# A fused attention kernel planned once and traced twice, with named buffers, planned tail jobs and sums spread by transposes

## The chip, the core and the metric

The kernel runs as one program on one core of a Trainium2 chip. The metric is device time in microseconds, lower is better. The core's engines run side by side, each through its own queue in order: TensorE (PE; its weight loads, PEld, have rows of their own), VectorE (DVE), ScalarE (ACT), GpSimd (POOL), and SyncE (SP), which here only issues DMAs.

## What is computed

Three layers follow each other: attention in which a query sees only the keys of its hash bucket, a causal attention with four experts of which two count per token, and a token mixer with a sine and a cosine. Everything is float32; the kernel splits each operand of a matmul into a high and a low part and multiplies high by high, high by low and low by high.

```python
def _attn_ref(q, k, v, proj):                      # 2 x 8 heads, 768 tokens, 64 wide
    ...                                            # 6 sign bits of q @ proj and k @ proj give buckets
    mask = q_bucket[:, :, :, None] == k_bucket[:, :, None, :]
    scores = scale * np.matmul(q, k.transpose(0, 1, 3, 2))
    scores = np.where(mask, scores, -1000000000.0)
    ...                                            # exp(scores - max)
    attn = attn / (np.sum(attn, axis=-1, keepdims=True) + 1e-09)
    return np.matmul(attn, v)

def _moe_ref(x, w_gate, wq, wk, wv, wo):           # x: (2, 768, 512), 4 experts, 2 of them per token
    ...
    for e in range(E):                             # q, k, v = x @ wq[e], x @ wk[e], x @ wv[e]
        ...                                        # causal softmax a, with the same division by its sums
        ye = a @ v @ wo[e]
        ...                                        # out += gate weight * ye

def _moe2_ref(x, w_theta, w_tok_r, w_tok_i, w_ch):
    theta = x @ w_theta
    zr, zi = x * np.cos(theta), x * np.sin(theta)
    u = x + np.einsum('ts,bsd->btd', w_tok_r, zr) + np.einsum('ts,bsd->btd', w_tok_i, zi)
    return u + np.maximum(u @ w_ch, 0.0)
```

## The kernel before

**Stages.** `attn_units` makes 12 units for each of 4 head pairs and each of 2 batches: a unit is 128 rows of scores of one head (`scores`, L861), their minimum and scaling on DVE (`low`, L870), the exponential on ACT (`exp`, L879), six to eight transposes on PE (`flip`, L887), the high part on ACT (`split_hi`, L898), the low part on DVE (`split_lo`, L901), and for two units together the product with V (`mix`, L917). `moe_units` makes 24 like them, causal and in four groups, with the projections of the experts between (`heads_a`, L1205; `value_rows`, L1140). A "group" is a head pair or an expert pair; there are 12.

**The spread of the sums.** When a group's exponentials are done, `scale` takes the reciprocals r (128 x 12) of the row sums, and POOL splits them into three bf16 parts (rs, L653 and L803, four instructions). `spread` transposes rs on PE (L816, bf16), ACT copies the 36 x 128 result (L818), and six bf16 matmuls with a constant of ones (`pick`, L820) lay the reciprocals out as 128 x 768 in PSUM. `finish` multiplies (L828).

**The tail.** From the end of the last group's units on, each of 12 token tiles (b, i) goes through `theta` and `out_proj` (L1389, six matmuls of 512 columns each), the range reduction (ACT L1421 and L1422, DVE L1423 to L1425; L1423 is the first and last reader on DVE that frees theta's PSUM tile), `trig`, `split_z` (zh, zl), and `mix` (L1493). `slab` brings weights for the mixer, with a decoding of 64-bit words on DVE (L674 to L676) for some. theta's and out_proj's PSUM tiles are called wk from (0, 2) on and have two buffers; ACT L1396 (`out_proj`'s copy x) frees the other one. `flip_u` and `channels` (L1401, L1413) end the program. POOL makes low parts (L701), the products with sine and cosine (L1433, L1434) and the sums of two halves (L811).

**What sets the order.** The code is a list of jobs. `Plan` reads the traced program, gives each instruction a price (`price`) and lists the instructions of each engine in an order by modelled times (`arrange`, shaken by the seeds of NUDGES). It is used twice: the first trace is planned with the order of the PSUM tiles ps left free; `sequence` turns it into an order of jobs up to the tail; the program is traced again in that order, planned again with all buffers going round in the order of the trace, and `fix` nails that second plan's order to each engine. The tail's jobs are traced in the order in which they are written. `busy` puts 38 filler matmuls (L765) into gaps of the first 20 us.

## Time and profile before

| | us |
|---|---|
| median of 3 timed runs (lowest to highest) | 558.03 (557.77 to 560.16) |
| the profiled execution | 552.84 |
| its span, first to last instruction | 551.0 |
| PE busy in it | 535.4 (3413 matmuls) |
| DVE, ACT, POOL busy in it | 438.8, 375.0, 291.7 |

The profiled execution is 5.2 us below the median. Matmuls are pipelined: a row's duration is that of one instruction from start to end, while what PE needs for it is the step to the next row's start. So the step is read from start times, and "busy" is a union of overlapping durations.

### The profile page before, as it was taken

To read this page: it belongs to the slowest core of one execution; us is meant where nothing else is said; L and a number is where in the kernel's file an instruction comes from. 1 tells how busy PE (TensorE), PEld (TensorE's weight loads), DVE (VectorE), ACT (ScalarE), POOL (GpSimd) and SP (SyncE) were. 2 spreads that over 40 slices of the span, in tenths; PEclk is the share of its full clock that TensorE was granted. 3 is DMA by queue.
4 is the path that set the end of the run, shared out by engine and by line. 5 is a ranking of instruction groups with operands and counts; after the bars stand their busy time and mean duration, and the time that the engine had idled before them with its cause. 6 is when DMAs were issued, how large, how long until landed. Compare 5 with 4: busy or idle time off the path is not lost.

```text
span 551.0 us, 9682 instructions
## 1 busy us (share of the span) xinstructions
PE 535.4 (97%) x3413; PEld 464.4 (84%) x3413; DVE 438.8 (80%) x723; ACT 375.0 (68%) x693; POOL 291.7 (53%) x286
## 2 busy tenths in 40 slices
PE   7999999999999999999999999979799999999997
PEld 4989998899889889899998988967588878788886
DVE  5888888898987898788895988889939799763343
ACT  6788887888764787678985757989356476563010
POOL 7957588648604758913121303846646576965000
PEclk9999999999999999999999999999899999999999
DMA  6744355426575766357561614533335442241012
GB/s 192 186 86 134 88 158 152 135 60 183 144 247 160 246 165 184 86 143 190 138 203 40 205 61 110 158 113 106 102 103 156 135 135 96 94 113 43 20 59 94
DMA packets 30367, 71.95 MB, mean 131 GB/s; under 512 B 4360, under 2 KB 6024, under 8 KB 30320
## 3 DMA queue, kind: packets, MB, share of 16 engines
q1 hardware_dynamic: 28160, 67.85, 43.5%
q10 hardware_dynamic: 2160, 3.50, 1.7%
q8 instruction: 27, 0.44, 0.3%
q14 instruction: 20, 0.16, 0.1%
HBM read 40.73 MB, written 14.16 MB: 100 GB/s over the span
## 4 chain that ended last, share of the span: by engine, by line
PE 78%; DVE 15%; ACT 3%; DMA 2%; issue 2%; ACTq 0%; SPq 0%; DVEq 0%
PE ps L861 16%; PE O L917 15%; PE ps L887 13%; PE ps L1493 12%; PE ps L1205 4%; PE wk L1413 3%; PE wk L1389 3%; PE ps L1413 3%; PE ps L1140 2%; PE ps L1068 2%; DVE g L676 2%; DVE ss L870 2%; DVE PTl L901 2%; DVE rr L1424 1%; DVE g L675 1%
## 5 line engine op out<-in xcount | busy, mean ns | idle before, releaser
L879 ACT ACTIVATE ss<-ss,m 128x768 f32<-128x768 f32 (+3 forms) x144 | 122.0, 848 | 22.6 <-DVE ss L870 21.8
L870 DVE TENSOR_SCALAR_CACHE_REDUCE ss<-ps 128x768 f32<-128x768 f32 (+3 forms) x144 | 119.2, 841 | 22.1 <-PE ps L861 14.6
L901 DVE TENSOR_TENSOR PTl<-ps,PTh 128x768 fp32r<-128x768 f32 x120 | 116.5, 980 | 15.1 <-ACT PTh L898 14.1
L898 ACT CAST PTh<-ps 128x768 fp32r<-128x768 f32 x120 | 98.1, 819 | 38.4 <-PE ps L887 35.8
L887 PE MATMUL ps<-ident,ss 128*128 128x128 f32 x744 | 111.0, 274 | 2.1 <-DVE PTl L901 2.0
L917 PE MATMUL O<-PTl,V 128*128 128x256 f32 (+1 forms) x384 | 104.5, 296 | 0.0
L917 PE MATMUL O<-PTh,V 128*128 128x256 f32 (+1 forms) x384 | 103.6, 293 | 0.8 <-ACT PTh L898 0.8
L887 PEld LDWEIGHTS ps<-ident,ss 128*128 128x128 f32 x744 | 85.0, 140 | 6.8 <-issue 2.6
L1493 PE MATMUL ps<-zh,tok 128*128 128x512 f32 x240 | 77.8, 395 | 0.2 <-ACT tok L698 0.2
L811 POOL TENSOR_TENSOR bt<-bt,ob 64x768 f32<-64x768 f32 x23 | 43.1, 1873 | 63.5 <-DMA bt<-ob 55.3
L917 PEld LDWEIGHTS O<-PTh,V 128*128 128x128 f32 x384 | 72.5, 189 | 3.9 <-ACT PTh L898 1.0
L917 PEld LDWEIGHTS O<-PTl,V 128*128 128x128 f32 x384 | 72.6, 190 | 2.5
L861 PE MATMUL ps<-op 76*128 76x256 f32 (+5 forms) x256 | 63.9, 342 | 1.8 <-ACT op L1006 1.6
L1493 PEld LDWEIGHTS ps<-zh,tok 128*128 128x128 f32 x240 | 44.8, 188 | 10.0 <-ACT tok L698 0.7
L1493 PE MATMUL ps<-zl,tok 128*128 128x512 f32 x120 | 45.9, 394 | 0.3 <-DVE zl L1445 0.3
L861 PEld LDWEIGHTS ps<-op 128*128 128x128 f32 (+1 forms) x256 | 40.0, 191 | 5.7 <-ACT op L1006 2.0
L701 POOL TENSOR_TENSOR tok<-raw,tok 128x512 fp32r<-128x512 f32 x27 | 40.3, 1497 | 6.1 <-ACT tok L698 5.7
L879 ACT ACTIVATION_READ_ACCUMULATOR ss<-ss,m 128x1 f32 x144 | 27.4, 190 | 0.0
L1493 PEld LDWEIGHTS ps<-zl,tok 128*128 128x128 f32 x120 | 22.5, 188 | 5.5 <-DVE zl L1445 0.7
L1433 POOL TENSOR_TENSOR kk<-kk,x 128x512 f32<-128x512 f32 x12 | 18.4, 1530 | 15.9 <-ACT kk L1432 8.4
L653 POOL TENSOR_SCALAR rs<-r 128x12 bf16<-128x12 f32 x24 | 5.4, 225 | 38.7 <-DVE r L947 21.6
L861 PE MATMUL ps<-skh,op 128*128 128x512 f32 x84 | 24.4, 358 | 0.7 <-issue 0.3
(241 smaller groups left out, 1150.0 us busy)
## 6 DMA issues: line engine op xcount, KB each, us to landing
raw<-in_wtok_dram SPq DMA_DIRECT2D x18, 512.0 KB
raw<-tok_d SPq DMA_DIRECT2D x27, 256.0 KB
bt<-ob SPq DMA_DIRECT2D x24, 192.0 KB
tok_d<-g SPq DMA_DIRECT2D x18, 256.0 KB
raw<-in_vP_dram SPq DMA_DIRECT2D x8, 384.0 KB
op<-qk_d SPq DMA_DIRECT2D x16, 192.0 KB
out_dram<-o ACTq DMA_DIRECT2D x11, 256.0 KB
raw<-in_qT_dram SPq DMA_DIRECT2D x7, 384.0 KB
```

Source lines behind the costliest of these rows:

```text
L701: nc.gpsimd.tensor_sub(l, raw, f(h))
L811: engine.tensor_add(self.bt[keep], self.bt[keep], self.ob[keep, side])
L861: nc.tensor.matmul(self.sp[:, c0:c1], lhs, rhs[:, c0 - off:c1 - off], start=a == 0, stop=last)
L870: i = nc.vector.tensor_scalar(self.ss[:, off:off + w], self.sp[:, off:off + w], -0.125, NEG, op0=OP.mult, op1=OP.min, accum_out=m)
L879: e = nc.scalar.activation(self.P[:, off:off + w], self.ss[:, off:off + w], AF.Exp, bias=m, scale=-1.0, accum_out=self.grp.den[:, side, i: ...
L887: nc.tensor.transpose(self.pt[:, j * 128:(j + 1) * 128], self.P[:, j * 128:(j + 1) * 128], ident)
L898: nc.scalar.copy(self.d[0], self.v)
L901: nc.vector.tensor_sub(self.d[1], self.v, f(self.d[0]))
L917: nc.tensor.matmul(o, g.V[:, j, side, :], rhs, start=j == 0 and a == 0, stop=j == w // 128 - 1 and a == 1)
L1205: nc.tensor.matmul(pp[:, c0:c1], lhs[:, kd, e, :], rhs[kd][:, c0:c1], start=n == 0, stop=n == 3 * NK - 1)
L1413: nc.tensor.matmul(o, lhs[:, sl], rhs[:, kd, cols], start=n == 0, stop=n == 3 * NK - 1)
L1493: nc.tensor.matmul(yp[t], lhs[:, a, t, :], rhs[:, a], start=i == 0 and a == 0 and n == 0, stop=i == NT - 1 and a == 1 and n == 2)
```

## The change

The program is planned once. A `Desk` counts the tiles that each job allocates; after the plan, `homes` gives each tile of a tag with more tiles than buffers the number of the buffer that the plan chose for it, and the second trace allocates it under a tag of its own with that number (`Pool.tile`). `fix` puts the first plan's order onto the second trace's instructions. The tail (`theta`, `out_proj`, `trig`, `split_z`, `slab`, `mix`, `flip_u`, `channels`, the opening of its pool) becomes jobs that `sequence` may move. Some prices and all NUDGES are new. `load_values` is a job of its own. The spread widens r on POOL into rb (128 x 768, float32) and transposes it with six float32 transposes; the transpose, the ACT copy, the POOL splits, `count` and `pick` are gone.

```diff
 NUDGES = [
-    (4000007, 402.2, 442.2, 300), (4000009, 440.6, 450.6, 1000), (4000016, 207.4, 247.4, 300),
...
-], [
-    (12000023, 40.3, 80.3, 300), (12000029, 0, 600, 100), (12000042, 117.9, 137.9, 100),
...
+    (1000006, 101.0, 181.0, 300), (1000018, 228.8, 308.8, 300), (1000108, 411.7, 421.7, 1000),
...
+class Desk:
+    def __init__(self, homes=None):
+        self.homes = homes or {}
+        self.job, self.count, self.made, self.starts = -1, 0, {}, {}
+    def begin(self, job, at):
+        self.job, self.count = job, 0
+        self.starts[job] = at
+class Pool:
...
+    def tile(self, shape, dtype, name, tag=None, bufs=1):
+        desk = self.desk
+        desk.count += 1
+        key = desk.job, desk.count
+        if key in desk.homes:
+            t = self.pool.tile(shape, dtype, name=name, tag=f"{tag}.{desk.homes[key]}", bufs=1)
...
         if n < 30:
-            s = 170 if o.kind != "InstReciprocal" else 240
+            s = 240 if o.kind == "InstReciprocal" else 450 if o.tiles[-1].startswith("den") else 170
...
         if len(o.w) > 1:
-            s = 82 + n * 1.045
+            return 82 + n * 1.045, 202 + n * 1.045
...
     s = 45 + n * 2.3 if o.kind == "InstTensorTensor" else 165 + n * 0.82
+    s += 150 if n < 30 else 0
...
+    def homes(self, t, made, reuse):
+        slot, used = {}, {}
+        def fresh(name):
+            if name not in slot:
+                slot[name] = used.setdefault(self.tag[name], 0)
+                used[self.tag[name]] += 1
+            return slot[name]
+        for old, new in reuse:
+            slot[new] = fresh(old)
...
-    def fix(self, tc, order):
+    def fix(self, nc, tc, order, waits, before, now):
...
+        def same(n):
+            k = bisect.bisect_right(starts, n) - 1
+            i = ins[n if k < 0 else n - starts[k] + now.starts[jobs[k]]]
...
         for line in order.values():
+            line = [same(n) for n in line]
             for a, b in zip(line, line[1:]):
-                tc.add_manual_dep(self.ops[b].ins, self.ops[a].ins.name, why, reason="order")
+                tc.add_manual_dep(b, a.name, why, reason="order")
...
-    count = const.tile([36, 2, NT], F32, name="count")
...
-    pick = const.tile([36, NT, 128], BF, name="pick")
...
-            r = r.rearrange("p h i -> p (h i)")
-            self.rs = pool.tile([128, 3, 2 * NT], BF, name="rs", tag="rs", bufs=2)
-            for n in range(2):
-                hi_pool(self.rs[:, n], r)
-                nc.gpsimd.tensor_sub(r if n == 0 else self.rs[:, 2], r, self.rs[:, n])
+            self.rb = pool.tile([128, NT, 2, D], F32, name="rb", tag="rb", bufs=1)
+            nc.gpsimd.tensor_scalar(self.rb,
+                                    r.rearrange("p h i -> p i h")[:, :, :, None].to_broadcast([128, NT, 2, D]),
+                                    1.0, 0.0, op0=OP.mult, op1=OP.add)
...
             self.rp = rp = ps_tile()
-            flat = rp.bitcast(BF)[0:36, 1792:1920]
-            nc.tensor.transpose(flat, self.rs.rearrange("p a c -> p (a c)"), identb)
-            rT = pool.tile([36, 128], BF, name="rs_T", tag="rs_T", bufs=2)
-            nc.scalar.copy(rT, flat)
             for i in range(NT):
-                nc.tensor.matmul(rp[:, i * 128:(i + 1) * 128], pick[:, i], rT, start=True, stop=True)
+                nc.tensor.transpose(rp[:, i * 128:(i + 1) * 128], self.rb[:, i].rearrange("p h d -> p (h d)"), ident)
...
-            if not first:
-                self.load_values()
...
+        at(s0 - (VAL0 if first else 16), pr.load_values)
...
+    def open_left():
+        s1.close()
+        late["pool"] = opened(ctx, name="p3", side="left")
+        late["wc"] = [late["pool"].tile([128, NK, DM], F32R, name="wc" + n) for n in "hl"]
...
-                    theta(*ahead)
+                    do(theta, *ahead)
                 if what == "o" and ahead:
-                    out_proj(*ahead)
+                    do(out_proj, *ahead)
...
+    for k in sequence or range(len(jobs)):
+        fn, args = jobs[k]
+        desk.begin(k, len(nc.cur_bb.bb.instructions))
+        families[k] = family(fn, args)
+        fn(*args)
...
-    line = None
-    for last in (False, True):
+    plan = line = None
+    desk = Desk()
+    while True:
...
-                waits, turns, stages = [], [], []
-                fused(tc, *args, waits, turns, stages, line)
-                plan = Plan(nc, tc, waits, turns, () if last else FREE)
-                t, order, _ = plan.arrange(SLACK, 6, NUDGES[last])
-                if not last:
-                    line = plan.sequence(t, stages)
-                    raise Draft
-                plan.fix(tc, plan.busy(t, order, 20e3))
+                waits, turns, families = [], [], {}
+                fused(tc, *args, waits, turns, desk, families, line)
+                if plan:
+                    plan.fix(nc, tc, order, waits, before, desk)
+                    break
+                plan = Plan(nc, tc, waits, turns, FREE)
+                t, order, reuse = plan.arrange(SLACK, 6, NUDGES)
+                homes = plan.homes(t, desk.made, reuse)
+                order = plan.busy(t, order, 20e3)
+                line = plan.sequence(t, reuse, desk, families)
+                before, desk = desk, Desk(homes)
+                raise Draft
```

The planner moves instructions; three places show how. In the lists of the kernel after, lines are its own: L846 is the new transpose, L943 is L917 of before, L887 is L861 of before, L1422 is L1389, L1447 to L1449 are L1423 to L1425, L705 to L707 are L674 to L676, L1469 is L1445, L841 is L811, L854 is L828.

PE, the end of the spread of the second group (batch 0, head pair 1), before (the bf16 transpose L816 stands 19 rows ahead, and four of the six L820 directly ahead):

```order
L887 MATMUL ps<-ident,ss 128x128 x3
L820 LDWEIGHTS pick
L820 MATMUL ps<-rs_T,pick 128x128
L887 MATMUL ps<-ident,ss 128x128 x2
L917 MATMUL O<-PTl,V 128x256
L917 MATMUL O<-PTh,V 128x256
L887 MATMUL ps<-ident,ss 128x128
L917 MATMUL O<-PTl,V 128x256
L820 LDWEIGHTS pick
L820 MATMUL ps<-rs_T,pick 128x128
L861 MATMUL ps<-op,sql 128x512
```

PE, the same spread after, whole:

```order
L943 MATMUL O<-PTl,V 128x256
L846 MATMUL ps<-ident,rb 128x128 x6
L943 MATMUL O<-PTh,V 128x256
L943 MATMUL O<-PTl,V 128x256
L887 MATMUL ps<-op,sql 128x512
```

What stood in two parts, of which the second was in three runs, stands in one run; over the program the 72 L820 stand in 21 runs, beside 12 single L816, and the 72 L846 in 19.

DVE, from the range reduction of theta (0, 2) to the read that frees theta (0, 3)'s PSUM tile, before (L1423 of (0, 2) stands directly ahead; the last row is that of (0, 3)):

```order
L1424 SCALAR_TENSOR_TENSOR rr<-kk,rr 128x512
L1425 TENSOR_SCALAR rr<-rr 128x512
L674 TENSOR_SCALAR g<-g 128x512
L675 SCALAR_TENSOR_TENSOR g<-raw,g 128x512
L676 SCALAR_TENSOR_TENSOR g<-raw,g 128x512
L811 TENSOR_TENSOR bt<-bt,ob 64x768
L1445 TENSOR_TENSOR z1l<-kk,z1h 128x512
L828 TENSOR_TENSOR y<-rT,bt 128x768
L1445 TENSOR_TENSOR z1l<-rr,z1h 128x512
L674 TENSOR_SCALAR g<-g 128x512
L675 SCALAR_TENSOR_TENSOR g<-raw,g 128x512
L1423 SCALAR_TENSOR_TENSOR rr<-kk,wk 128x512
```

DVE, the same after; ahead of these rows stand L1447 of (0, 2) and then L707, L1448, L705 and L1469:

```order
L706 SCALAR_TENSOR_TENSOR g<-raw,g 128x512
L1469 TENSOR_TENSOR z1l<-rr,z1h 128x512
L707 SCALAR_TENSOR_TENSOR g<-raw,g 128x512
L1449 TENSOR_SCALAR rr<-rr 128x512
L841 TENSOR_TENSOR bt<-bt,ob 64x768
L854 TENSOR_TENSOR y<-rT,bt 128x768
L705 TENSOR_SCALAR g<-g 128x512
L706 SCALAR_TENSOR_TENSOR g<-raw,g 128x512
L707 SCALAR_TENSOR_TENSOR g<-raw,g 128x512
L1469 TENSOR_TENSOR zl<-kk,zh 128x512
L1469 TENSOR_TENSOR zl<-rr,zh 128x512
L1447 SCALAR_TENSOR_TENSOR rr<-kk,wk 128x512
```

From one such read to the next there are 12 instructions before and 16 after; from (0, 3)'s to (0, 4)'s there are 9 before and 6 after.

PE, the first use of the wk buffer that DVE frees after theta (0, 3), with the semaphores that an instruction waits for, before (wk_5283 is theta (0, 4), in the bank that theta (0, 3) had):

```order
L1493 MATMUL ps_5162<-z1l_5147,tok_5109 128x512
L1493 MATMUL ps_5162<-z1h_5146,tok_5110 128x512
L1493 MATMUL ps_5175<-z1h_5146,tok_5109 128x512 [waits Activation_49]
L1493 MATMUL ps_5162<-z1h_5146,tok_5109 128x512
L1389 MATMUL wk_5283<-wth_4586,yh_4660 128x512 [waits DVE_49]
L1389 MATMUL wk_5283<-wtl_4587,yh_4660 128x512
```

After (wk_5254 is out_proj (0, 4), in the bank that theta (0, 3) had; theta (0, 4), wk_5220, has the bank that out_proj (0, 3) had, which ACT frees):

```order
L1422 MATMUL wk_5220<-wth_4527,yl_4625 128x512
L1508 MATMUL ps_5070<-zl_5191,tok_5103 128x512 [waits DVE_49]
L1508 MATMUL ps_5083<-zh_5190,tok_5103 128x512 [waits Activation_49]
L1508 MATMUL ps_5039<-zl_5191,tok_5103 128x512
L1508 MATMUL ps_5039<-zh_5190,tok_5104 128x512
L1508 MATMUL ps_5039<-zh_5190,tok_5103 128x512
L1508 MATMUL ps_5039<-zl_5191,tok_5103 128x512 [waits DVE_49]
L1422 MATMUL wk_5254<-woh_4525,yh_4624 128x512 [waits DVE_49]
```

From theta (0, 2)'s last matmul up to the one that waits for that bank, PE has 87 matmuls before and 118 after.

## Rows read from the trace of the kernel before

**Rows 1.** The page: PE's busy time, and the chain that ended last by engine.

```profile
PE 535.4 (97%) x3413; PEld 464.4 (84%) x3413; DVE 438.8 (80%) x723; ACT 375.0 (68%) x693; POOL 291.7 (53%) x286
...
PE 78%; DVE 15%; ACT 3%; DMA 2%; issue 2%; ACTq 0%; SPq 0%; DVEq 0%
```

**Rows 2.** Busy time by stretch; columns in the first line.

```profile
core 0: us, PE busy (x) PEld busy (x) DVE busy (x) ACT busy (x) POOL busy (x), PEclk, DMA share, GB/s
0.00:10.00 10.00, 7.20 (x29) 3.42 (x30) 5.16 (x20) 5.54 (x10) 6.22 (x14) 1.00 0.61 216
...
360.00:380.00 20.00, 16.92 (x104) 13.43 (x103) 17.17 (x27) 17.75 (x33) 7.86 (x9) 1.00 0.32 108
380.00:400.00 20.00, 16.15 (x64) 12.68 (x63) 19.84 (x18) 10.19 (x19) 14.71 (x9) 0.91 0.31 88
...
440.00:460.00 20.00, 19.73 (x86) 15.85 (x85) 18.49 (x22) 14.08 (x25) 14.07 (x10) 1.00 0.30 93
```

**Rows 3.** PE's waits: who, for whom, us in total, times, longest.

```profile
PE wk L1389 <- DVE rr L1423: 3.8, 1, 3.8
PE ps L887 <- DVE PTl L901: 2.0, 1, 2.0
```

**Rows 4.** Timeline of PE around one spread: start us, duration us, instruction, count.

```profile
194.11 0.28 PE L917 MATMUL O<-PTh,V 128*128 128x256 f32 x1
194.32 0.23 PE L816 MATMUL ps<-identb,rs 128*36 128x128 bf16 x1
194.48 0.38 PE L917 MATMUL O<-PTl,V 128*128 128x256 f32 x1
194.70 0.28 PE L917 MATMUL O<-PTh,V 128*128 128x256 f32 x1
...
195.06 0.38 PE L887 MATMUL ps<-ident,ss 128*128 128x128 f32 x2
195.37 0.51 PE L820 MATMUL ps<-rs_T,pick 36*128 36x128 bf16 x6
195.81 0.66 PE L887 MATMUL ps<-ident,ss 128*128 128x128 f32 x4
```

**Rows 5.** Timeline of PE: a single L820 between transposes, and a run of six.

```profile
84.24 0.55 PE L887 MATMUL ps<-ident,ss 128*128 128x128 f32 x3
84.72 0.23 PE L820 MATMUL ps<-rs_T,pick 36*128 36x128 bf16 x1
84.88 0.44 PE L887 MATMUL ps<-ident,ss 128*128 128x128 f32 x2
...
201.90 0.82 PE L887 MATMUL ps<-ident,ss 128*128 128x128 f32 x6
```

**Rows 6.** POOL's and ACT's part of a spread, a 128 x 768 POOL copy, from groups and timelines.

```profile
L653 POOL TENSOR_SCALAR rs<-r 128x12 bf16<-128x12 f32 x24 | 5.4, 225 | 38.7 <-DVE r L947 21.6
...
364.53 0.26 ACT L818 COPY rs_T<-ps 36x128 bf16<-36x128 bf16 x1
...
13.70 0.83 POOL L653 TENSOR_SCALAR sqh<-raw 128x768 fp32r<-128x768 f32 x1
```

**Rows 7.** Timelines of PE and DVE, 359 to 396 us.

```profile
374.79 0.40 PE L1389 MATMUL wk<-wth,yl 128*128 128x512 f32 x1
...
359.88 1.94 DVE L1425 TENSOR_SCALAR rr<-rr 128x512 f32<-128x512 f32 x1
...
377.07 0.43 DVE L1425 TENSOR_SCALAR rr<-rr 128x512 f32<-128x512 f32 x1
377.42 0.68 DVE L1423 SCALAR_TENSOR_TENSOR rr<-kk,wk 128x512 f32<-128x512 f32 x1
...
395.95 0.68 DVE L1423 SCALAR_TENSOR_TENSOR rr<-kk,wk 128x512 f32<-128x512 f32 x1
```

**Rows 8.** Timeline of SP near the start: DMA issues.

```profile
2.12 0.43 SPq L969 DMA_DIRECT2D raw<-in_qT_dram  x1
...
10.63 0.46 SPq L1091 DMA_DIRECT2D skh<-skh  x1
```

More of the change, by code (lines that the diff above doesn't have):

```diff
@@ L540, in arrange, with sequence @@
         return self.forward(rank.tolist(), slack, hold=HOLD)
-    def sequence(self, t, stages):
-        starts = [s[0] for s in stages]
-        count = len(stages) - 1
-        of = [0] * len(self.ops)
-        for o in self.ops:
-            k = bisect.bisect_right(starts, o.n) - 1
-            of[o.n] = k if 0 <= k < count else None
-        pre = [set() for _ in range(count)]
+    def homes(self, t, made, reuse):
[7 more added lines that the diff above has]
+            slot[new] = fresh(old)
+        many = [key for key, (bufs, names) in self.tags.items() if len(names) > bufs]
+        homes = {made[name]: fresh(name) for key in many for name in self.tags[key][1]}
+        taken = {new for _, new in reuse}
+        self.last = max((n for key in many if key.startswith("O_") for n in self.tags[key][1] if n not in taken),
+                        key=lambda n: min(t[k] for k in self.enter[n]))
+        homes.update((made[name], slot[self.last]) for name in made if name.startswith("spare"))
+        return homes
+    def sequence(self, t, reuse, desk, families):
+        jobs = sorted(desk.starts)[:-1]
+        starts = [desk.starts[k] for k in jobs]
+        ends = starts[1:] + [desk.starts[len(jobs)]]
+        of = [bisect.bisect_right(starts, o.n) - 1 for o in self.ops]
+        pre = [set() for _ in jobs]
         def edge(a, b):
-            if a is not None and b is not None and a < b:
+            if a >= 0 and b >= 0 and a != b:
                 pre[b].add(a)
@@ L592, in sequence @@
                     heapq.heappush(heap, (when[j], j))
-        assert len(line) == count
+        assert len(line) == len(jobs), "the jobs wait for one another"
         return line
@@ L598, in busy @@
         line, ops = order["PE"], self.ops
-        waits = [[t[b] - t[a] - ops[a].step, b, 0] for a, b in zip(line, line[1:]) if t[b] < until]
+        until = min(until, min(t[n] for n in self.enter[self.last]))
+        waits = [[t[b] - t[a] - ops[a].step, b, 0] for a, b in zip(line, line[1:]) if t[b] <= until]
         step = ops[self.spare[0]].step
@@ L1416, in theta @@
     def theta(b, i):
-        th = late["work"]()
+        th = work((b, i) < (0, 2))
         project(th, b, i, "wt")
@@ L1552, in fused @@
                     if c > 1:
-                        channels(b, c - 2)
-                    flip_u(b, c)
-    late["work"] = lambda: ps_tile()[:, :DM]
+                        do(channels, b, c - 2, False)
+                    do(flip_u, b, c, False)
     b = B - 1
```

159 lines of the change are left out of this document (85 added, 74 removed), and 67 rows, old and new, of the table NUDGES.

## The prediction, made before the kernel after was run

> **What bounds the kernel now.** The page first: PE is busy for 535.4 of 551.0 us and holds 78% of the chain that ended last, with DVE next at 15% [rows 1]. So time comes off in two ways only: PE gets less to do, or PE waits less. The busy share cannot tell these apart, since overlapping durations hide small gaps; so I read steps from start to start in the timeline, and the stretches for the waits. The stretches show 3.1 us of PE idle in 360 to 380 and 3.9 in 380 to 400, where the granted clock also fell to 0.91, while DVE was busy for 19.84 of 20 us; in 440 to 460 PE takes 86 matmuls, nearly all of 512 columns, in 19.73 us, 0.23 each [rows 2]. The list of PE's waits names the two large ones: 3.8 us for DVE L1423, 2.0 us for DVE L901 [rows 3]. Before 360 us the waits that show are at the start, where PE is busy for 7.20 of the first 10 us [rows 2].
>
> **The spread, on PE.** Before, from row to row: the matmul ahead of L816 takes 0.21 in place of 0.12 (half the 0.23 of 512 columns), L816 itself 0.16, the one after it 0.22 in place of 0.12: 0.35 together. The six L820: the two transposes ahead take 0.31 in place of 0.22, the run 0.44, and the block behind it loses about 0.06 [rows 4]; 0.59 together, so 0.94 for a spread in one run, 11.3 for twelve. But the 72 L820 stand in 21 runs, nine more than needed. A single one costs 0.48 - 0.33 for three delayed transposes plus 0.16 for itself, 0.31 [rows 5], of which 0.06 is already counted: nine times 0.25 is 2.3. Sum before 13.6 us, all on PE, which sets the end. After: 72 transposes of 128 x 128 float32. A run of two lasts 0.38 [rows 4], one of six 0.82 [rows 5]: four steps more, 0.11 each; 72 x 0.11 = 7.9, and a run's ends cost nearly nothing, because the step behind the last transpose is short and the next one long by as much. Gain 13.6 - 7.9 = 5.7. Bounds: 3.4 if the nine extra runs cost nothing (11.3 - 7.9), 6.2 if each costs its whole 0.31. I take 5.7, nearest to the rows that show both forms.
>
> Here a rule of the Trainium skill speaks against the change. Runs of float32 transposes go at 0.11 a step in the rows [rows 4, 5], and 360 to 380 us, which holds one of eight, has a granted clock of 1.00 [rows 2]. The Trainium skill, page "TensorE: Matmul & The Clock Gate", section "Part 4: PE-mode transpose", says that a transpose took about 275 ns in a kernel and does not count as busy work for the clock. By its figure the 72 would be an estimated 19.8 us and the spread a loss of 6.2. The trace disagrees for the step, and shows no fall of the clock by such a run.
>
> **The spread, elsewhere.** POOL had four instructions of about 0.22 each; it gets one of 0.83, the price of a 128 x 768 copy [rows 6]: even, 0.9 against 0.8. ACT loses 12 x 0.26 [rows 6]. The chain from r to the spread loses the trip PE, ACT, PE; it was hidden behind other matmuls, so nothing but slack. Where POOL runs, DVE instructions whose operands all lie in SBUF stretch: L1425 took 0.43 at 377 us and 1.94 at 360 us [rows 7]. One rb of 0.83 can hold a DVE instruction longer than one of 0.22 did, at worst 12 x 0.6 = 7 us on DVE; DVE has slack outside 340 to 400, where two rb stand, so 0 to 1.2 on the path, and I take 0. `count` and `pick` go from the start: nothing, PE waits there for data.
>
> **Where the tail begins.** Before, theta (0, 4) took the bank of theta (0, 3) and waited for DVE L1423. PE reached it 21.9 us after theta (0, 2)'s last matmul, 3.8 of it waiting; DVE needed 18.5 us for the 12 instructions from one L1423 to the next, 1.54 each, against 0.68 for that instruction alone [rows 3, 7]. The clock then lost up to 9% of 20 us, 1.8 [rows 2]; say 5.3 in all. After, theta (0, 4) takes the bank that ACT frees, and the first to wait for that read is out_proj (0, 4), 118 matmuls on instead of 87: 104 x 0.23 + 14 x 0.12 = 25.6 us. But DVE now has 16 instructions in the place of 12: at 1.54 each 24.6, after the 2.6 from PE's last matmul to the first L1423, and 0.7 for the last [rows 7]: 27.9, so 2.3 late; at 0.68 each, not late at all. The next one is closer: theta (0, 5) needs the read of theta (0, 4), six DVE instructions later (4.1 to 9.2 us), and has 15 matmuls, 3.5 us, between: late by 0.6 to 5.7. DVE is not stretched all the way, as POOL runs dry; I take 1.5 and 0.8, no fall of the clock (the 2.0 us wait at 360 left it at 1.00 [rows 2, 3]). Gain 5.3 - 2.3 = 3.0, bounds -2.7 and 5.3.
>
> At 360 us PE waited 2.0 for an L901 that stood behind a stretched L1425 [rows 3, 7]. The plan after puts that L1425 behind two reads of scores and one L901 more. That leaves one stretched L1424 in the chain instead of two: gain 1.0, bounds 0 and 2.0.
>
> **The start.** The second head pair's q and k were issued at 2.12 us; now they stand on SP behind three moves, the last of which went out at 10.63 [rows 8]. First use was at 13.70 on POOL [rows 6]. At the 216 GB/s of the first 10 us [rows 2] 0.8 MB takes 3.6 us, so k lands near 15 and PE's hash of that pair may wait a little: loss 0.5, bounds 0 and 3. `load_values` as a job of its own moves the V loads; they land far ahead of their use: 0.
>
> **The rest of the order.** Named buffers add no instruction. Everything else is a new order of the same work; the trace shows no large wait in 20 to 340 or after 400 us to win, and a new order may bring some: 0, bounds -2 and +4.
>
> **How the numbers follow.** 5.7 + 3.0 + 1.0 - 0.5 = 9.2 off. On the profiled execution, 551.0 of span and 1.8 around it, that is 552.84 - 9.2 = 543.6. The median of the timed runs is 5.2 higher, at 558.03; the same difference gives **548.8**. A measurement tells 0.5%, 2.8 us, from no change.
>
> Case 1, the sum within about 4 us: 545 to 553, chance 0.56.
>
> Case 2, the tail's start loses all its waits (3.1 + 3.9 us and the clock's 1.5) and the spread gives its 6.2: 13 to 15 off, 542 to 545, chance 0.12. For: PE needs only DVE to keep 1.1 us per instruction there. Against: the read after next has 3.5 us of cover.
>
> Case 3, PE's gain is waited away: PE arrives sooner, but DVE and POOL do as much as before, and between 360 and 400 they set the time, not PE. Then the spreads of the last two groups give nothing and the waits for L1423 come back at their bound, 5.7 + 2.3, with the clock's 1.5 again: 5.7 + 1.0 - 0.5 - 1.0 - 9.5 + 5.3 = about 1 off, 554 to 559, chance 0.17. DVE at 19.84 of 20 us speaks for it [rows 2].
>
> Case 4, slower: the b = 0 tiles stay bound by DVE and POOL to 460 us. DVE does 22 instructions in 18.49 us in 440 to 460, 0.84 each [rows 2]; up to 0.91 each PE would not see it; at 1.2 each 22 take 26.4, 6.4 more than the stretch, and two such stretches cost 13, 4 more than all gains: from 561, and up to 570, chance 0.09. It decides if POOL runs without a pause there; before, its busy time was 14.07 of 20.
>
> Case 5, the transposes of the spread pull the clock down to its lower level, 1.2 GHz: 0.22 a step, 72 x 0.22 = 15.8 against 13.6, so 2 lost instead of 5.7 won: 556 to 557, chance 0.02. The page named above would have it so.
>
> Case 6, the change doesn't do what it says: the second trace's named buffers make waits that the plan did not know, and the order is kept by PE at the price of those; 1 to 3 us back of case 1, 551 to 555, chance 0.04.
>
> Faster by over 0.5% (below 555.2): 0.56 + 0.12 + 0.04 and a third of case 3, **0.77**. Within: the rest of case 3 and case 5, **0.14**. Slower: **0.09**. The range **542 to 557** leaves out half of case 3, case 4 and the far sides of the others.
>
> **What would show it.** The timeline of a spread: runs of L846 at 0.11, no pause ahead of them; PE's summed steps down by 5 to 6 us in 0 to 350. Waits of PE: theta (0, 4) none, out_proj (0, 4) and theta (0, 5) some 2 us for DVE, clock 1.00 in that stretch. Near 21 us a short wait for POOL. The prediction is wrong if a wait of over 3 us stands where none was, or if the spread's transposes wait for rb.

## The result

The changed kernel took 540.41 us (median of 4 runs, 539.64 to 541.77), the kernel before 558.45 beside it (557.77 to 560.16): ratio 0.9675, 95% interval 0.9644 to 0.9707. That is 18.0 us off, where 9.2 were forecast and 542 was the range's lower end. Its profiled execution took 540.96 us (span 539.2) and stands among its timed runs. Before, the profiled execution stood 5.2 us below the median. Between the two profiled executions the gain is 11.9 us, so 6 of the 18 us are in neither profile.

The page of the changed kernel, busy time (engine, us, share of the span, instructions) and the chain that ended last, as in [rows 1]:

```profile
PE 528.5 (98%) x3401; PEld 467.7 (87%) x3401; DVE 441.5 (82%) x722; ACT 371.6 (69%) x681; POOL 290.6 (54%) x249
...
PE 82%; DVE 11%; DMA 3%; issue 2%; ACT 1%; SPq 0%; ACTq 0%; DVEq 0%
```

Some of its stretches, as in [rows 2] (us; busy time and instructions of PE, PEld, DVE, ACT, POOL; granted clock, DMA share, GB/s):

```profile
0.00:10.00 10.00, 8.37 (x31) 4.30 (x32) 6.36 (x19) 5.72 (x10) 4.87 (x12) 1.00 0.44 141
...
260.00:280.00 20.00, 18.34 (x136) 16.79 (x135) 17.72 (x40) 14.76 (x34) 3.65 (x2) 0.91 0.50 145
...
360.00:380.00 20.00, 19.87 (x109) 16.74 (x108) 16.85 (x24) 15.93 (x28) 10.88 (x9) 1.00 0.33 86
380.00:400.00 20.00, 20.00 (x88) 16.16 (x87) 19.59 (x20) 13.81 (x25) 14.77 (x10) 1.00 0.40 118
...
440.00:460.00 20.00, 19.76 (x89) 16.05 (x88) 19.50 (x22) 13.71 (x25) 16.29 (x11) 1.00 0.45 136
```

What PE waited for, as in [rows 3] (total us, times, longest):

```profile
PE ps L887 <- DVE PTl L927: 2.0, 2, 1.7
PE ps L887 <- DVE ss L896: 1.2, 1, 1.2
PE ps L788 <- DVE warm L792: 1.2, 1, 1.2
PE wk L1422 <- DVE rr L1447: 0.7, 1, 0.7
PE ps L1229 <- DVE x L854: 0.6, 1, 0.6
PE ps L887 <- DVE r L973: 0.5, 1, 0.5
```

Where the tail begins PE hardly waits: 19.87 and 20.00 us busy in place of 16.92 and 16.15, the clock at 1.00 in both stretches, though DVE is about as full as before (19.59 of 20). The wait of 3.8 us for L1423 is gone; the line that answers to it, L1447, has 0.7. New are 1.7 us for an L927 at 266 us and 1.2 for an L896 at 343 us. Behind the one at 266 the granted clock fell here too: it is 0.91 in 260 to 280, which is up to 1.8 us.

To set work against waits I took PE's steps from start to start. The work in a step is the median, in the trace of before, of the steps between the same kinds of instruction; what a step takes beyond that is wait, and a lower clock counts as wait too. In us, with the waits split at the last product with V, where the tail is left alone:

| profiled execution | work | waits up to there | waits behind |
|---|---|---|---|
| before | 524.9 | 14.5 | 7.2 |
| after | 517.8 | 14.6 | 2.3 |

So the two profiles show 7.1 us less work and 4.9 less waiting in the tail. Each holds one stretch of 20 us at a clock of 0.91, up to 1.8 us that counts as wait: before in the tail (380 to 400), after ahead of the split (260 to 280). Without these the tail's waits fell by 3.1 and those ahead of it by 1.7. How finely the kinds are told apart moves work against wait: with kinds by shape and type, taken two in a row, the gain in work is 5.3 us, taken three in a row 7.5; the sums and the waits behind hardly move (7.7 and 2.9 in place of 7.2 and 2.3). So a difference of work is known to some 2 us. This table is continued below.

### The profile page after: what moved, and what is told of

The parts are those of the page before. It is cut to its first block, busy times and chain, and to the rows that moved or that the text cites. A ratio compares the mean times of both kernels' runs of the same rounds, so it can differ in the third digit from the quotient of the medians.

```text
span 539.2 us, 9655 instructions
## 1 busy us (share of the span) xinstructions
PE 528.5 (98%) x3401; PEld 467.7 (87%) x3401; DVE 441.5 (82%) x722; ACT 371.6 (69%) x681; POOL 290.6 (54%) x249
## 4 chain that ended last, share of the span: by engine, by line
PE 82%; DVE 11%; DMA 3%; issue 2%; ACT 1%; SPq 0%; ACTq 0%; DVEq 0%
PE ps L1508 15%; PE ps L887 15%; PE O L943 15%; PE ps L913 13%; PE ps L1229 4%; PE wk L1422 4%; PE wk L1437 4%; PE ps L1437 3%; PE ps L1164 3%; PE ps L1092 2%; DVE ss L896 2%; DVE g L706 2%; DVE g L705 1%; PE ps L846 1%; DVE PTl L927 1%
## 5 line engine op out<-in xcount | busy, mean ns | idle before, releaser
L896 DVE TENSOR_SCALAR_CACHE_REDUCE ss<-ps 128x768 f32<-128x768 f32 (+3 forms) x144 | 119.0, 840 | 19.1 <-PE ps L887 14.6
L927 DVE TENSOR_TENSOR PTl<-ps,PTh 128x768 fp32r<-128x768 f32 x120 | 116.2, 979 | 10.6 <-ACT PTh L924 9.9
L913 PE MATMUL ps<-ident,ss 128*128 128x128 f32 x744 | 109.8, 274 | 0.6 <-DVE ss L896 0.3
L943 PE MATMUL O<-PTh,V 128*128 128x256 f32 (+1 forms) x384 | 103.5, 293 | 0.0
L943 PE MATMUL O<-PTl,V 128*128 128x256 f32 (+1 forms) x384 | 103.5, 295 | 0.0
L1508 PE MATMUL ps<-zh,tok 128*128 128x512 f32 x240 | 78.9, 394 | 0.0
L841 POOL TENSOR_TENSOR bt<-bt,ob 64x768 f32<-64x768 f32 x23 | 43.2, 1878 | 60.6 <-DMA bt<-ob 29.7
L943 PEld LDWEIGHTS O<-PTh,V 128*128 128x128 f32 x384 | 72.8, 190 | 1.9 <-ACT PTh L924 0.3
L943 PEld LDWEIGHTS O<-PTl,V 128*128 128x128 f32 x384 | 72.8, 190 | 1.7
L887 PE MATMUL ps<-op 76*128 76x256 f32 (+5 forms) x256 | 63.5, 345 | 4.1 <-DVE PTl L927 2.0
L887 PEld LDWEIGHTS ps<-op 128*128 128x128 f32 (+1 forms) x256 | 41.0, 194 | 8.2 <-DVE PTl L927 2.4
L831 POOL TENSOR_SCALAR rb<-r 128x768 f32<-128x768 f32 x12 | 10.0, 834 | 59.0 <-DVE r L973 31.8
L706 DVE SCALAR_TENSOR_TENSOR g<-raw,g 128x512 uint32<-128x512 uint32 x26 | 25.6, 986 | 0.5
L707 DVE SCALAR_TENSOR_TENSOR g<-raw,g 128x512 uint32<-128x512 uint32 x26 | 25.5, 979 | 0.5
```

Source lines behind the costliest of these rows:

```text
L706: nc.vector.scalar_tensor_tensor(gu, words[:, :, 0], 29, gu, op0=OP.logical_shift_right, op1=OP.bitwise_or)
L841: engine.tensor_add(self.bt[keep], self.bt[keep], self.ob[keep, side])
L887: nc.tensor.matmul(self.sp[:, c0:c1], lhs, rhs[:, c0 - off:c1 - off], start=a == 0, stop=last)
L896: i = nc.vector.tensor_scalar(self.ss[:, off:off + w], self.sp[:, off:off + w], -0.125, NEG, op0=OP.mult, op1=OP.min, accum_out=m)
L913: nc.tensor.transpose(self.pt[:, j * 128:(j + 1) * 128], self.P[:, j * 128:(j + 1) * 128], ident)
L927: nc.vector.tensor_sub(self.d[1], self.v, f(self.d[0]))
```

## Experiments

### The missing 6 us: the kernel before once more

**The kernel before, unchanged.**

> The kernel before, unchanged, timed and profiled once more. In the first measurement its profiled execution took 552.84 us and its timed ones 557.77 to 560.16. Theory A (the profiled execution was a lucky one; something in before varies or waits by about 5.5 us in most executions): timed runs near 558 again, and a profiled execution near 558 too, which then shows one wait or one stretch at a lower granted clock of about 5 us that the first profile lacks. Theory B (being profiled shortens this kernel, by whatever): timed near 558, profiled near 553 again, spans of the timed runs 5 us above the profiled one's. If timed runs come to 553 here, the difference was the chip's and the ratio of the two kernels is nearer 0.977 than 0.9675.

Measured: 555.76 us (10 runs, 554.60 to 558.14) and 556.06 for 18 more runs beside it, 552.03 to 559.71. The mean granted clock of PE goes with the time: the quickest run of the 18 (552.03) had 0.997, those near 555 had 0.987 to 0.991, and 559.58 and 559.23 had 0.981; 0.016 of clock goes with 7.6 us. It isn't the whole of the scatter, for 0.984 stands beside 557.07 and beside 559.71. The first profiled execution, at 0.996, was one of the quickest that this kernel has. The first four timed runs, 558.45, lay high themselves: in this and the later groups of runs before took 555.8 to 557.1, so some 2 of the 18 us are the draw. The clock of those four runs is not on record; in the groups where it is, all but one of the runs over 557.7 had 0.981 to 0.988. The profile of this run has the same two waits, 2.0 and 3.8 us, and a lower clock behind both:

```profile
360.00:380.00 20.00, 17.45 (x89) 13.57 (x90) 14.30 (x26) 14.90 (x29) 4.43 (x8) 0.83 0.18 60
380.00:400.00 20.00, 16.16 (x66) 12.78 (x66) 19.80 (x16) 11.37 (x20) 16.24 (x10) 0.96 0.32 102
400.00:420.00 20.00, 20.00 (x85) 16.22 (x85) 10.10 (x13) 11.44 (x21) 11.73 (x9) 0.96 0.33 106
```

In the timeline of PE (start us, us, instruction, idle before it) the step of a product of 512 columns is 0.23 ahead of the wait and 0.43 for some 3 us behind it, the lower of the clock's two levels (1.2 GHz), then 0.23 again:

```profile
393.29 0.40 PE L1493 MATMUL ps<-z1l,tok 128*128 128x512 f32 x1
393.52 0.86 PE L1493 MATMUL ps<-z1h,tok 128*128 128x512 f32 x3
398.23 0.80 PE L1389 MATMUL wk<-wth,yh 128*128 128x512 f32 x1 [3.84 <-DVE rr L1423]
398.82 0.63 PE L1389 MATMUL wk<-wtl,yh 128*128 128x512 f32 x1
399.24 0.63 PE L1389 MATMUL wk<-wth,yl 128*128 128x512 f32 x1
...
402.68 0.39 PE L1493 MATMUL ps<-z1l,tok 128*128 128x512 f32 x1
402.91 0.39 PE L1493 MATMUL ps<-z1h,tok 128*128 128x512 f32 x1
```

So Theory A holds as to the scatter, though its 558 did not come, neither timed nor profiled (554.60), and the forecast's step "the same difference" is an error. By the granted clock this profile loses 0.17, 0.04 and 0.04 of 20 us, 5.0; the first lost 1.8.

**The waits filled, order kept.** The program is traced a third time, and the order of the second plan is put onto it with these extra products:

```diff
+        self.fill = {3817: 17, 4099: 16}   # instruction's number in the program: repeats ahead of it
```

> The kernel before with its order kept on every engine, and its two large waits of PE filled: 17 repeats of a V product (128 x 256) ahead of the wait at 360 us and 16 repeats of a token product (128 x 512) ahead of theta (0, 4), so PE is busy where it waited, and nothing becomes earlier. The repeats are added into the sums, so those sums hold one product 17 or 18 times. Theory A (the clock, which fell after these waits in most executions, is the 4 to 5 us by which before's executions differ): mean granted clock 0.996 or more in every run, times 551 to 553, no run over 555, where the kernel before beside it shows 552 to 560. Theory B (the spread of before's times has another cause): 556 as before, the same scatter, or up to 3 slower since the repeats cost themselves.

Measured: 551.29 us (9 runs), 0.9913 of the kernel before (0.9883 to 0.9943), which took 557.12 beside it. Its clock was 0.991 to 1.000, at 0.997 or more in seven of nine runs; before had 0.981 to 0.991. Nothing became earlier but the steps behind the waits:

```profile
360.00:380.00 20.00, 18.84 (x116) 15.07 (x115) 17.17 (x28) 17.33 (x33) 7.86 (x10) 1.00 0.28 94
380.00:400.00 20.00, 19.85 (x86) 15.75 (x85) 19.80 (x18) 10.72 (x19) 14.46 (x9) 1.00 0.33 93
```

That is Theory A in the main: 5.8 us by the medians, 4.8 by the ratio, were the clock that fell after the waits. Theory A wanted every run at 0.996 or more and none over 555; two went to 554.5 and 555.4, at 0.991 and 0.994, so the fillers don't keep it up every time. The Trainium skill, page "TensorE: Matmul & The Clock Gate", section "Part 1: The HAM clock gate", names idleness of PE as what halves its clock; the runs agree, with the clock up when the waits are filled and a step of 0.43 for 0.23 behind a wait that isn't.

**A wait added to the changed kernel, order kept.**

```diff
+        if desk.homes and (b, i) == (0, 3):
+            waits.append((held[b, i][0].ins, held[b, i - 1][1].ins))   # first matmul of theta, last L1449
```

> The changed kernel with its order kept on every engine and one wait added that its planner does not know: theta (0, 3) on PE waits for the last DVE step of theta (0, 2) (L1449), which in the profile ended 4.0 us after PE got there. Theory A (a wait of 4 us here costs its length and then the clock): 540.4 + 4.0 + 1.5 to 4 = 546 to 548.5, mean granted clock 0.99. Theory B (only the length): 544 to 545, clock 0.997 or more. Theory C (the tail has slack elsewhere, later waits shrink): 540 to 542.

Measured: 542.98 us (6 runs), clock 0.997 to 1.000. The wait came out at 2.7 us, since PE got there 1.1 us later than in the profile of after (380.98 for 379.86) and DVE's step ended no later. Behind it the step is 0.22 to 0.23:

```profile
380.75 0.40 PE L1514 MATMUL ps<-z0l,tok 128*128 128x512 f32 x1
383.86 0.50 PE L1424 MATMUL wk<-wth,yh 128*128 128x512 f32 x1 [2.71 <-DVE rr L1453]
384.20 0.39 PE L1424 MATMUL wk<-woh,yh 128*128 128x512 f32 x1
384.42 0.39 PE L1514 MATMUL ps<-z0h,tok 128*128 128x512 f32 x1
```

It cost 2.6 by the medians, about its own length, and 4.7 by the ratios to before (0.9759 against 0.9675). The clock is Theory B's; the time lies between B's 544 to 545 and Theory C's 540 to 542. A wait of 2.7 us left the clock alone in this profile. In before the one of 2.0 at 361 us, with one of 0.8 behind it, lowered it in one of two profiles, and in the profile of after one of 1.7 did (0.91 in 260 to 280). What decides that, these runs don't show.

### Which part of the change is it

**The new spread alone, in the kernel before; the old spread alone, in the kernel after.** The edits are the two pieces of the spread (`scale` and `spread`) in the diff of the change, put into the kernel before and taken back in the kernel after.

> The kernel before with the new spread alone (one POOL copy that widens r, six transposes); two plans, shared buffers and the tail's written order stay as they were, and the planner orders the work anew. Theory 1 (the spread's PE steps are worth what the rows say, 5.7 to 7 us, and the planner's new order is neutral): 551 to 553, ratio 0.988 to 0.990. Theory 2 (the spread carries the whole 18 us, since PE also lost time to the trip PE, ACT, PE): about 541 to 544. Theory 3 (the nudges were sought for one program, and another program loses their worth): over 556, in spite of the cheaper spread.

> The changed kernel with the old spread alone put back (four POOL instructions, a transpose, an ACT copy, six matmuls of 36 rows); one plan over the whole, named buffers and planned tail stay, ordered anew by the planner. Theory 1: 546 to 548, the spread's 5.7 to 7 us back. Theory 2 (the spread carries nearly all): 555 to 558. Theory 3 (nudges belong to their program): over 550, with the excess in waits and not in PE's steps.

Measured: 571.21 us (ratio 1.0253, 1.0191 to 1.0315) and 561.21 (1.0075, 1.0048 to 1.0103): both worse than either kernel. By steps the work is as the spread says, 519.0 with the new and 524.9 with the old; the waits are 42.7 and 29.0 in place of before's 21.7 and after's 16.9. This speaks for Theory 3: a list of nudges belongs to its program. So the parts are compared with the lists emptied:

```diff
-NUDGES = [ ... ]
+NUDGES = []        # the kernel before: [], []
```

> The changed kernel with its list of nudges emptied: the same instructions and prices, the planner's order without the seeds found for it. It measures what such an order is worth by itself. Theory 3 (the order found by seeds is a large part of the 18 us): 550 or more. Theories 1 and 2 (the parts carry it, the seeds only polish): 541 to 546, PE's steps unchanged.

> The kernel before with the new spread, as in the run that took 571, and with both lists of nudges emptied. If foreign nudges did the harm there (Theory 3): 555 or less. If two plans with shared buffers cannot give a good order for this program whatever the seeds: 560 or more, waits spread from 20 to 470 us as there.

> The changed kernel with the old spread, as in the run that took 561, and with the nudges emptied; its counterpart with the new spread and no nudges took 541.5. If foreign nudges did the harm: 547 to 550 (PE's 7 us back and little else). If the old spread itself makes waits (its trip PE, ACT, PE, and four POOL steps where one stands): 555 or more.

> The kernel before with both lists of nudges emptied: the last cell of a table of old or new spread against two plans or one, all without nudges (new and two plans 541.2, new and one plan 541.5, old and one plan 551.9). Theory S (the spread alone is the change, plans and named buffers bring nothing): 550 to 554. Theory P (old spread and two plans are bad together): 558 or more. If it is near 552 and without the fall of the clock, then the nudges of before themselves cost it some 5 us on the chip.

| without nudges | old spread | new spread |
|---|---|---|
| two plans, shared buffers, tail as written | 553.27 (551.69 to 555.47) | 541.23 (540.00 to 544.93) |
| one plan, named buffers, planned tail | 551.93 (550.89 to 554.75) | 541.49 (540.56 to 543.01) |

That is Theory S; the changed kernel without nudges stayed within the 541 to 546 of Theories 1 and 2, and the old spread with one plan fell between what its two theories gave. The columns differ by 12.0 and 10.4 us (11.3 and 10.9 by the ratios to before), the rows by nothing that can be measured in the right column (0.9741, 0.9692 to 0.9790, and 0.9722, 0.9682 to 0.9761) and by 1.3 us in the left (0.9944 and 0.9917). In these orders the spread is the gain; the plan made once, the named buffers, the tail's jobs and the new prices together bring nothing that shows. A cell is one order of the planner, and a random nudge moves it by 5 to 6 us (below), so some us either way from them are not excluded. The nudges of after are worth 1.1 us, no more than runs scatter; those of before cost it 0.6% (its ratio without them is 0.9944, 0.9914 to 0.9975): that order has the two waits behind which the clock fell, to 0.981 to 0.991 in nearly all its runs, against 0.994 to 0.997 without the nudges.

The stretch 380 to 400 us of the upper row's two kernels, old spread and then new:

```profile
380.00:400.00 20.00, 17.45 (x69) 13.71 (x68) 19.66 (x15) 10.35 (x19) 16.70 (x10) 0.91 0.42 130
```

```profile
380.00:400.00 20.00, 20.00 (x88) 16.30 (x87) 19.08 (x19) 12.56 (x22) 13.36 (x10) 1.00 0.31 92
```

With DVE about as full in both, PE waits in the one and its clock is lower, and in the other neither.

### What PE pays for a spread

**Both forms, added to the changed kernel with its order kept.** Ahead of each spread, into the same bank:

```diff
+    # first kernel: the six transposes once more
+                for i in range(NT):
+                    nc.tensor.transpose(rp[:, i * 128:(i + 1) * 128], self.rb[:, i].rearrange("p h d -> p (h d)"), ident)
+    # second kernel: the old form, from constants
+                nc.tensor.transpose(rp.bitcast(BF)[0:36, 1792:1920], identb[:, 0:36], identb)
+                for i in range(NT):
+                    nc.tensor.matmul(rp[:, i * 128:(i + 1) * 128], identb[0:36], identb[0:36], start=True, stop=True)
```

> The changed kernel with its order kept and the six transposes of each spread done twice (72 more transposes of 128 x 128, into the same place, the output unchanged). If PE sets the end all along, and a step in such a run is 0.11 us, it takes 540.4 + 7.9 = 548.3. If much of PE's work there lies beside other waits: 541 to 545. If a transpose costs more than its step in a run: 550 or more.

> The changed kernel with its order kept and PE's part of the old spread done as well ahead of each new one: a bfloat16 transpose to 36 rows and six bfloat16 products of 36 rows, in one run, from constants, into the bank that the new spread then overwrites; they wait for nothing, the output is unchanged. By the rows one such group costs 0.75 to 0.94, so 9 to 11.3 for twelve: 549.4 to 551.7. Less the run with doubled transposes this is the spread's gain on PE's steps alone, 1.1 to 3.4 by these numbers if nothing is said of the nine extra runs, against 10.4 between the kernels with old and new spread without nudges: what is missing would be the trip PE, ACT, PE and its waits. If it comes to 556 or more, PE's steps carry the gain by themselves.

Measured: 547.23 and 546.75 us, 6.8 and 6.3 more than the changed kernel (by the ratios to before, 0.9831 and 0.9828 against 0.9675, 8.7 and 8.5). PE's work grew by 7.9 and 8.2, and its waits gave back 3 in the profiled executions (16.9 to 13.7 and 13.5); up to 1.8 of that is the lower clock of 260 to 280 us, which only after's profile has of these three. So most of what PE gets to do there shows in the time, and the old form in one run costs about what the new one does; the 9 to 11.3 expected of it were too much. In the timeline of the second kernel, one bf16 transpose and the six products go in 0.60 us, 0.07 a product, and the two transposes behind them take 0.19 in place of the 0.14 of a row of after (219.77 below):

```profile
223.77 0.28 PE L960 MATMUL O<-PTl,V 128*128 128x256 f32 x1
223.98 0.23 PE L858 MATMUL ps<-identb 128*36 128x128 bf16 x1
224.14 0.51 PE L860 MATMUL ps<-identb 36*128 36x128 bf16 x6
224.58 0.44 PE L863 MATMUL ps<-ident,rb 128*128 128x128 f32 x2
224.77 0.37 PE L960 MATMUL O<-PTh,V 128*128 128x256 f32 x1
```

The same place in after, for [rows 4, 5]:

```profile
219.77 0.38 PE L846 MATMUL ps<-ident,rb 128*128 128x128 f32 x2
219.91 0.37 PE L943 MATMUL O<-PTh,V 128*128 128x256 f32 x1
220.11 0.60 PE L846 MATMUL ps<-ident,rb 128*128 128x128 f32 x4
220.47 0.36 PE L943 MATMUL O<-PTl,V 128*128 128x256 f32 x1
```

What the old form cost beyond that, in before, is that it was torn: its transpose stands alone, because the products wait for ACT, and the products stand in 21 runs, each of which PE enters and leaves at a price. Other traces agree. In four kernels with the old form the 72 products stand in 21 runs (before), 18 (random nudge, below), 17 (no nudges) and 12 (one plan, no nudges), and their work is above that of their counterparts with the new spread by 7.1, 6.8, 6.5 and 4.7 us: some 0.27 for each extra run (0.09 and 0.24 by the two other ways to tell kinds). The 4.7 are left with no extra run, where only the twelve transposes stand alone.

The Trainium skill's 275 ns for a transpose (page "TensorE: Matmul & The Clock Gate", section "Part 4: PE-mode transpose") are no price here. A single one in before does last 0.27 from start to end:

```profile
85.40 0.27 PE L887 MATMUL ps<-ident,ss 128*128 128x128 f32 x1
```

But they overlap, and 72 more cost 6.8 us, or 8.7 by the ratios, 95 to 121 ns each, with the clock at 1.000 in every run. The 19.8 us that the prediction worked out from that figure took a duration for a step.

### The waits of the tail

**The new spread in two groups of twelve, or in the other ten**, in the kernel before without nudges:

```diff
+            self.wide = last        # the two groups of the second mixture; the other kernel: not last
...
+            if self.wide:           # rb and six transposes, else the four POOL steps and the old form
```

> The kernel before without nudges, with the new spread in two of its twelve groups only, the two of the second mixture, which end at the tail's start. Old spread in all took 553.3, new in all 541.2; by PE's steps and waits some 6 us of the 12 lie ahead of the tail and 5 in its waits. Theory T (the tail's waits hang on the spreads that end there): 553.3 - 5 - 1 = 547 to 548.5, and the waits behind the last attention product fall from 7.7 to about 2.5. Theory L (the loss is shared out evenly, a twelfth each): 551 to 552, waits in the tail as before. Theory R (each new order falls its own way): anything, not the sum with the run beside it.

> The counterpart: the new spread in the first ten groups, the old one in the two of the second mixture. Theory T: 553.3 - 5 = 547.5 to 549, waits in the tail 7 as before. Theory L: 543 to 544, waits in the tail half gone. Theory R: the two gains of this run and the one beside it don't add up to 12.

Measured: 547.03 (546.85 to 547.36) and 549.76 us (548.76 to 551.91), 6.2 and 3.5 off 553.27. The tail's waits were 3.4 and 8.0, the work 522.5 and 520.2. That looked like Theory T, the second time being 0.8 over its range; but the two gains add up to 9.7 and not to 12, which is Theory R's sign. The next two took the old spread apart in those two groups:

```diff
     # first kernel, in those two groups: no transpose, no ACT copy
-            nc.tensor.transpose(flat, self.rs.rearrange("p a c -> p (a c)"), identb)
-            nc.scalar.copy(rT, flat)
-                nc.tensor.matmul(rp[:, i * 128:(i + 1) * 128], pick[:, i], rT, start=True, stop=True)
+                nc.tensor.matmul(rp[:, i * 128:(i + 1) * 128], pick[:, i], identb[0:36], start=True, stop=True)
     # second kernel, in those two groups: one POOL step for four
+                hi_pool(self.rs, r.rearrange("p h i -> p (h i)")[:, None, :].to_broadcast([128, 3, 2 * NT]))
```

> The kernel before without nudges (553.3), and in the two groups of the second mixture the old spread without its transpose and its ACT copy: the six products of 36 rows stay, from constants, so they wait neither for POOL's four steps nor for ACT; that y is not scaled by its sums. With the new spread in these two groups it took 547.0 and the tail's waits fell from 7.7 to 3.4. Theory V (the chain POOL, PE, ACT, PE ahead of the products is what pushes the tail's work into waits): 546.5 to 548.5, tail's waits 4 or less. Theory F (the form of the products, their seven steps on PE): 552 to 553, tail's waits 7 or more.

> The kernel before without nudges (553.3), and in the same two groups one POOL step in place of the four that split the sums (all three parts hold the upper one, so that spread comes out about threefold); transpose, ACT copy and products stay. Theory P (POOL's four steps, in the stretch where POOL and DVE are both busy, make the tail's waits): 547 to 549, tail's waits 4 or less. Otherwise 552 to 553.5, tail's waits 7 or more.

Measured: 549.85 us (549.42 to 551.98) with waits of 6.6 behind the last product with V, and 550.13 (549.87 to 550.52) with 3.8. The times are the same, both between the two ranges that were given. The waits look different, but up to 1.8 us of the 6.6 are a lower clock, which the tail of the second profile doesn't have; the stretch 380 to 400 us of the first and the second:

```profile
380.00:400.00 20.00, 17.96 (x71) 14.13 (x71) 19.73 (x17) 10.92 (x19) 15.92 (x10) 0.91 0.46 137
```

```profile
380.00:400.00 20.00, 20.00 (x88) 16.23 (x87) 18.02 (x17) 11.99 (x21) 15.16 (x10) 1.00 0.34 103
```

The profiled execution of the first was also its slowest, 551.98 at a clock of 0.996; its other three took 549.4 to 550.1 at 0.999 or more. So Theory V is not borne out (without the chain the waits are above its 4 even so), and for Theory P there is only one profile, with a time 1 above its 547 to 549 and 1.4 more of PE's work in the new order. Each of these is one order of the planner, so the last pair asked what an order's chance weighs:

```diff
-NUDGES = [], []
+NUDGES = [(7000001, 0, 600, 300)], [(7000002, 0, 600, 300)]
```

> The kernel before (old spread) with one made-up nudge for each plan in place of the lists: every instruction's rank moved at random by up to 300 ns. Without nudges it took 553.3, waits behind the last attention product 7.7. Theory S (the 12 us between old and new spread hold for orders of this planner in general): 551 to 557, and 10 or more above the run beside it. Theory R (what falls on an order by chance is as large as that difference): under 549, or over 560.

> The same made-up nudges with the new spread; without nudges 541.2, waits behind the last attention product 2.6. Theory S: 540 to 545. Theory R: 548 or more, or tail's waits of 6 and more with the new spread too.

Measured: 558.45 us (556.79 to 561.88) and 547.25 (547.03 to 548.52). The difference between old and new spread stands, 11.2. But each rose by 5 to 6 through one random nudge, out of Theory S's ranges (551 to 557, 540 to 545), and the new spread's tail waited 7.9 us, more than the old one's 6.9, which is Theory R's sign; what PE waits for there is again DVE's work for the tail (the list of its waits):

```profile
PE ps L1427 <- DVE z1l L1379: 2.3, 1, 2.3
...
PE wk L1323 <- DVE rr L1357: 1.6, 1, 1.6
```

So the tail's waits don't belong to the spread. The table of steps, in us:

| kernel (profiled execution) | work | waits up to the last product with V | waits behind |
|---|---|---|---|
| old spread, two plans, no nudges | 524.5 | 13.8 | 7.7 |
| new spread, two plans, no nudges | 518.0 | 13.1 | 2.6 |
| old spread, one plan, no nudges | 522.3 | 19.4 | 6.7 |
| new spread, one plan, no nudges | 517.6 | 15.5 | 2.6 |
| old spread, two plans, random nudge | 524.7 | 20.0 | 6.9 |
| new spread, two plans, random nudge | 517.9 | 16.4 | 7.9 |

Work falls by 6.5, 4.7 and 6.8 in the three pairs. The waits fall in all three too, by 5.8, 8.0 and 2.6, but at other places each time. Part of that is the clock: the old spread without nudges has one stretch of 20 us at 0.91 with two plans and two with one plan, its counterparts none, and with the random nudge both have one. At up to 1.8 us each, at least 4.0, 4.4 and 2.6 are left. Why the waits fall is not settled; that POOL's four steps make them is not shown.

## Why the prediction was wrong in size

**The step that failed** is the last: "The median of the timed runs is 5.2 higher, at 558.03; the same difference gives 548.8". It makes 5.8 of the 8.4 us by which the forecast missed, since the changed kernel's median is 0.55 below its profiled execution. The other 2.6 are the sum itself: on the profiled execution it said 543.6, and the changed kernel's took 540.96. The 5.2 us were no constant: most of them were the clock behind the two waits, lower in most executions than in the one profile that was read, and filling these waits took 4.8 to 5.8 us off. For the three runs themselves the clock is not on record. The prediction had both halves in hand: it priced the clock at 1.8 us behind one wait and at nothing behind the other, as that execution had it [rows 2], and left the 5.2 unexplained. With them counted as clock, the sum gives 543 to 544, which the measurement still undercuts by 3.

**The spread on PE.** Forecast 5.7, bounds 3.4 and 6.2. Measured in work: 7.1 between the two kernels (5.3 to 7.5 by other kinds), 6.5, 6.8 and 4.7 in the pairs. The new form is worth its 7.9 (72 more of them brought 7.9 of work). The old one comes to 15.0, 7.9 + 7.1, where the rows gave 13.6, and that is within what the choice of kinds moves. That it costs by being torn, not by its form, is what the rows said (nine extra runs at 0.25, the lone transpose), and the added run of 8.2 and the count of runs, 0.27 for an extra one (0.09 to 0.27 by the kinds), agree with it. The 11.3 for spreads in one run held twelve lone transposes.

**Where the tail begins.** Forecast a gain of 3.0, the clock's 1.5 in it; the waits behind the last product with V fell by 4.9, up to 1.8 of it clock, and in most executions of before more of the clock comes on top. The two waits expected at out_proj (0, 4) and theta (0, 5), 1.5 and 0.8, did not come. The reason given, the bank that ACT frees, is not needed for it: two plans with the tail as written had 2.6 us of waits as well, and the new spread with a random nudge 7.9.

**The wait at 360 us** went, a gain of 2.0 where 1.0 was forecast; new waits at 266 and 343 us and the lower clock behind the first took it back, so the waits up to the last product with V are the same, 14.5 and 14.6. **The start** lost nothing: PE was busy for 8.37 of the first 10 us against 7.20 [rows 2]. But the first 20 us held 1.8 us of waits in before's profile and 0.8 in its repeat, 1.9 in after's and 3.6 in that with the added wait, so the 0.5 forecast is below what one execution can tell. **The rest of the order** was put at 0, bounds -2 and 4: in the profile the other waits ahead of the tail rose by about the 2.0 that the one at 360 us gave, up to 1.8 of it the clock behind the wait at 266; the random nudge, at 5 to 6, shows that the bounds were narrow.

**Rivals.** Case 2, with 13 to 15 off, was the nearest. Case 3 (PE's gain waited away) and case 4 (DVE and POOL as the bound) did not come, though case 4 was close: in 440 to 460 DVE took 0.89 us an instruction (19.50 for 22), where 0.91 was its point. Case 5 is out by the doubled transposes. Case 6, at 551 to 555, did not come; whether the named buffers made any of the new waits, no run here tells, and together with the single plan they brought nothing that shows.

## What to carry to other kernels

Where the profiled execution is not among the timed ones, find out why before adding the difference as a constant: compare the granted clock of every run, for a wait of PE can cost once by its length and once more by the clock behind it, in some executions only. Price an operation on PE by how it must stand, not by its form: a trip to another engine in its middle tears it apart, and its lone transposes and split runs are what the old form cost PE here beyond the new one. And where a planner orders the program, compare edits with its tuned list emptied and in more than one order; a list tuned for one program cost the other 9 to 30 us, and a random nudge 5 to 6.

## What was not expected of the hardware

The same program with the same two waits, 2.0 and 3.8 us, ran with a mean granted clock from 0.981 to 0.997, 7.6 us apart, and a wait of 2.7 us added to the other kernel left it at 0.997 and more, while one of 1.7 us in that kernel's own profile was followed by a clock of 0.91 in its stretch. Six bf16 products of 36 rows in one run go at 0.07 us each, faster than a float32 transpose at 0.11.
